# Attention and feed-forward layer on one core: the pooled result added to the windows by GpSimd's accumulating transfers instead of a load and a tensor_add, with the planner's durations and leads set anew

## The chip, the core and the metric

The program runs on one core of a Trainium2 chip. A core has a matrix engine (TensorE, PE in the profile), a vector engine (VectorE, DVE), a scalar engine (ScalarE, ACT), GpSimd (POOL), a queue engine that only issues transfers (SyncE, SP), and 16 DMA engines that carry the transfers. Each engine runs its own list of instructions in order; engines wait for one another through semaphores alone. The metric is the device time of the whole program in microseconds; less is better.

## The reference

```python
# q, k, v: (B=8, H=8, S=576, D=64)
q_d, k_d, v_d = (a.reshape(B, H, 144, 4, D).mean(axis=3) for a in (q, k, v))
out_up    = np.repeat(softmax(q_d @ k_d.T / 8) @ v_d, 4, axis=2)              # pooled attention
out_local = softmax(where(|i - j| < 4, q @ k.T / 8, -1e6)) @ v                # local attention
x  = (out_up + out_local).transpose(0, 2, 1, 3).reshape(B, S, 512)
xn = (x - mean) / sqrt(var + 1e-6) * g_ln                                     # layer norm
return x + relu(xn @ w_ch1) @ w_ch2                                           # 512 -> 2048 -> 512
```

The weights come as 64-bit floats (the program reads them as pairs of 32-bit words); the rest is fp32.

## The kernel before

**The stages.** Local attention is cut into 40 windows, 5 per batch, of 128 rows each (two stretches of 64). Pooled attention runs per batch in two halves of four heads. Where both are there, `norm(i)` makes a window's rows of x, normalizes them and turns them, and nine blocks of 512 rows (`blocks`) go through the feed-forward. The weights do not stay on chip as a whole: in a first stage ("visits" 0 to 8, one per block of rows) five eighths of the hidden width are computed by plain products, in a second stage (visits 9 to 17) the rest, by seven products in place of eight. Attention runs beside the first stage. Visit 0 also decodes the first stage's weights, and batch 0's attention comes ahead of it.

**Matmuls in three.** Each fp32 product is done as three on halves: a rounded high half (`hi`, ScalarE's cast, L407) and the rest (`lo`, VectorE's subtraction, L413 in `halved`). In the down projection (L1303, tile `acc`) the three are high weight x low activation, low weight x high, high x high. The weights' 64-bit words are first put together by `words`: ScalarE L376, VectorE L384 (`low_word`) and L387, then `halved`. A weight's `low` tile thus needs L384, L387 and L413 on VectorE before PE can use it; for w_ch2 in the first stage these are the 10 tiles `low20_0` to `low20_9`, 128 hidden columns each. `acc0_0` and `acc0_1` are the two halves (256 rows each) of visit 0's block.

**The pooled result.** `pooled(b)` loads raw tiles of q, k and v on SP (L819), GpSimd adds their groups of four rows (L832, L833), PE and the others do the attention. For batches 1 to 7 `keep` (L968) writes the result, each row four times, to the tensor `ud` in DRAM by two GpSimd transfers. (Batch 0 goes another way, through PE at L1039 and VectorE at L1048.)

**A window's norm, batches 1 to 7 (35 windows).** SP loads the window's rows of `ud` into a tile `up` (`load_up`, L1026, two transfers of 64 x 512); GpSimd adds it to the local result (`plus`, L1045, xl += up); VectorE takes the statistics (`stats`, L1052, L1054, L1055); GpSimd raises the variance to -1/2 (`rstd`, L1058, tile `mv`); VectorE normalizes (`normed`, L1062, tile `xn`); PE turns (L1070, tile `px`); ScalarE scales into the block (L1093); GpSimd writes x out for the end (`spill`, L1099, to `xs`).

**What sets the order.** `Plan` is a list scheduler that runs when the program is built. A task is added with an engine, a listed duration, a due time, what it depends on and what room it takes (`add`, L42); `order()` (L55) then takes tasks greedily by their due time as the listed durations let them begin, and so writes each engine's instructions in a fixed order. On the chip nothing of the listed times is left, only the order and the semaphores. A task with `ahead=n` may not be listed more than n us before its due time; `AHEAD` is that bound for the raw tiles' loads. `due` comes from constants such as `T0` (start of visit 0), `SHORT` (length of a second-stage visit) and `PRIOR` (how long before its batch the pooled part is due).

Of the kernel before, what the change touches and what calls it, by code (L numbers as in the profile page):

```python
# [14 lines left out]
ALU = mybir.AluOpType  # L15
# [7 lines left out]
class Plan:  # L23
# [17 lines left out]

    def add(self, eng, dur, fn, deps=(), due=0.0, take=(), give=(), lag=None, ahead=1e9, alt=None, kb=0, n=1, more=0.1, late=None):  # L42

        opts = {eng: (dur, fn, 0.0)}
        if alt is not None:
            opts[alt[0]] = alt[1:]
        t = SimpleNamespace(
            n=len(self.tasks), opts=opts, dur=dur, deps=[d for d in deps if d is not None],
            due=due, take=take, give=give, lag=lag, ahead=ahead, open=0.0, waits=0, eng=None, fn=None, kb=kb, pieces=n, more=more,
            late=late if late is not None else self.late if eng == "SP" else 0.0,  # L50
        )
        self.tasks.append(t)
        return t

    def order(self):  # L55
# [40 lines left out]
        while left:  # L96
# [61 lines left out]
def attention_then_ffn(  # L158
# [115 lines left out]
    STAGE = [sum(VISITS[i][0] != VISITS[i - 1][0] for i in range(1, v + 1)) for v in range(len(VISITS))]  # L274
    T0 = 36
    LONG0, LONG, SHORT = 75, 73, 34
    LENGTH = [LONG0 if v == 0 else LONG if FIRST[c] == v else SHORT for v, (_, c) in enumerate(VISITS)]
# [21 lines left out]
    W_NORM, G_NORM = 2.0, 9.0  # L299
    PRIOR = 30  # L300
    START = 0
# [14 lines left out]

    B0W, B0W_GAP, B0G, B0G_GAP = 5, 3, 12, 1.5
    AHEAD = 45
    U_SPARE = 4
# [21 lines left out]
    def dve(n):  # L341
        return 0.06 + n / 950.0

    def pool(n):
        return 0.13 + 0.0022 * n

    BEGUN = 1.0

# [6 lines left out]
    def words(g, which, f, due):  # L355
# [38 lines left out]
        t = add("ACT", 0.87, high_word, (t,), due)  # L394
        return add("DVE", 1.26, low_word, (t,), due, give=(("u", 2),))

    def halved(get, name, deps, more, due, keep, n=512, room=U, gone=U):

        x = SimpleNamespace()
        add = plan.add  # L400

        def high():
            x.a = get()
            if keep.get("hi") is None:
                keep["hi"] = unit([P, 512], f"hi{name}", F32R)
            x.hi = keep["hi"]
            nc.scalar.copy(x.hi[:, x.a[1]], x.a[0].bitcast(F32)[:, x.a[1]])  # L407

        def low():
            a, cols = x.a  # L410
            if keep.get("lo") is None:
                keep["lo"] = unit([P, 512], f"lo{name}", F32R)
            nc.vector.tensor_sub(keep["lo"][:, cols], a.bitcast(F32)[:, cols], x.hi.bitcast(F32)[:, cols])  # L413

        t = add("ACT", act(n, True), high, deps, due, take=room)
        return add("DVE", dve(n) * 1.4, low, [t] + more, due, take=room, give=gone)

# [134 lines left out]
    def local(i):  # L552
# [44 lines left out]
        for src, nm in () if own else ((q, "q"), (k, "k")):  # L597
# [20 lines left out]
            else:  # L618
# [9 lines left out]
                for jb in range(2):  # L628
                    ts.append(add("SP", 1.95, lambda src=src, nm=nm, jb=jb: load_blocks(src, nm, jb, nc.sync), ts,
                                  due - 14.0, take=() if jb else U, lag=LAT, kb=200, n=4, more=0.8, ahead=AHEAD,  # L630
                                  alt=("ACT", 3.2, lambda src=src, nm=nm, jb=jb: load_blocks(src, nm, jb, nc.scalar), LATER) if i >= ALSO else None))
# [236 lines left out]
    def pooled_pair(b, hg, pr, x, ready):  # L868
# [126 lines left out]
        if own or pr == 0:  # L995
            return
        t = add("POOL", 2 * BEGUN, keep, x.od_done, due, lag=LAT, kb=640, n=2, more=0.6)
        ud_done.setdefault(b, []).append(t)
# [14 lines left out]
    def norm(i):  # L1013
# [7 lines left out]

        def load_up():
            x.up = unit([P, DM], f"up{i}")
            for par in range(2):
                t0 = window_start(w, par)
                nc.sync.dma_start(x.up[64 * par : 64 * par + 64], ud[b][t0 : t0 + 64])  # L1026

# [4 lines left out]
        def expand():  # L1032
            x.up = psa(f"ex{i}")
            for hg in range(2):
                es = slice(hg * 256, (hg + 1) * 256)
                for par in range(2):
                    for c in cover(par):
# [4 lines left out]
                        )  # L1042

        def plus():
            nc.gpsimd.tensor_add(xl(), xl(), x.up)  # L1045

# [423 lines left out]
```

## Time and profile before

| what | value |
|---|---|
| runs | 1038.08, 1036.22, 1039.69 us, median 1038.08 |
| the profiled execution | 1032.09 us, its span 1030.4 us |
| mean granted TensorE clock of the profiled execution | 0.996 of full speed |
| busy share of the span | PE 98%, VectorE 64%, ScalarE 44%, GpSimd 45% |

The profile is one execution, 0.6% under the median of the runs. The span runs from the first to the last instruction; about 1.7 us lie around it. Busy time of an engine says how long its instructions were at work; where an instruction stood for a semaphore, the trace names the instruction or transfer that released it. A granted clock of 1.00 is 2.4 GHz, 0.50 is 1.2 GHz.

### The profile page before, as it was taken

The numbers are of one execution on the slowest core, as the hardware profiler recorded it, in microseconds if no ns is written. First come the engines' busy times: TensorE is split into PE (matmuls) and PEld (weight loads), VectorE is DVE, ScalarE is ACT, GpSimd is POOL, SyncE is SP. The second block draws the span as 40 slices with busy tenths as digits, with TensorE's granted clock in tenths as the row PEclk, the third lists the DMA queues.
The fourth block names the chain that finished last, engine by engine and source line by source line (L and its number), as shares of the span: only waits on it lengthen the run. The fifth ranks groups of instructions, "written<-read, shape, count | busy, mean of one in ns | idle before, by whom it ended". The sixth has DMA issues, their size and how long they took to land. (4 is left out here: it accounts for less than half of the span.)

```text
span 1030.4 us, 23083 instructions
## 1 busy us (share of the span) xinstructions
PE 1008.4 (98%) x8332; PEld 854.5 (83%) x8332; DVE 664.1 (64%) x1559; ACT 449.3 (44%) x1408; POOL 463.2 (45%) x538
## 2 busy tenths in 40 slices
PE   9899989998999999999999999999999999999998
PEld 8678868887877888888888887888888999989897
DVE  6899976665765465566666554573595576556743
ACT  6587636364353464353362353653342233321311
POOL 4453567685667655664643222441244223443112
PEclk9999989999999999999999999999999999999999
DMA  7899878877878668677666241331245422344312
GB/s 181 222 271 246 197 146 217 188 185 182 200 167 198 185 141 189 150 195 162 133 175 134 74 137 60 130 135 55 86 147 184 164 91 101 137 164 164 118 63 108
DMA packets 272786, 159.24 MB, mean 155 GB/s; under 512 B 196032, under 2 KB 241344, under 8 KB 272672
## 3 DMA queue, kind: packets, MB, share of 16 engines
q1 hardware_dynamic: 249056, 119.86, 45.9%
q0 software_dynamic: 12736, 36.59, 10.5%
q10 hardware_dynamic: 10880, 1.31, 0.9%
q8 instruction: 66, 1.08, 0.4%
q14 instruction: 48, 0.39, 0.1%
HBM read 111.68 MB, written 46.01 MB: 153 GB/s over the span
## 5 line engine op out<-in xcount | busy, mean ns | idle before, releaser
L1303 PE MATMUL acc<-hiw,hl 128*128 128x512 f32 x576 | 234.5, 407 | 0.0
L1303 PE MATMUL acc<-low,hh 128*128 128x512 f32 x576 | 226.0, 392 | 5.0 <-DVE low L413 5.0
L1303 PE MATMUL acc<-hiw,hh 128*128 128x512 f32 x576 | 225.5, 392 | 0.0
L1303 PEld LDWEIGHTS acc<-hiw,hh 128*128 128x128 f32 x576 | 108.4, 188 | 24.1
L1303 PEld LDWEIGHTS acc<-low,hh 128*128 128x128 f32 x576 | 108.9, 189 | 23.0 <-DVE low L413 5.7
L1303 PEld LDWEIGHTS acc<-hiw,hl 128*128 128x128 f32 x576 | 108.6, 189 | 19.8
L1385 POOL TENSOR_TENSOR back<-back,back 128x512 f32<-128x512 f32 x36 | 48.1, 1348 | 171.1 <-DMA back<-parts 122.3
L1240 ACT ACTIVATE hh<-h 128x256 fp32r<-128x256 f32 x180 | 59.4, 386 | 144.9 <-PE h L1232 127.5
L1232 PE MATMUL h<-hix,hiw 128*128 128x512 f32 x360 | 109.5, 399 | 0.0
L1247 DVE SCALAR_TENSOR_TENSOR hl<-h,hh 128x256 fp32r<-128x256 f32 x180 | 66.9, 414 | 65.6 <-ACT hh L1240 65.2
L1283 ACT ACTIVATE hh<-e 128x256 fp32r<-128x256 f32 x108 | 39.0, 410 | 143.0 <-DVE e L1264 77.9
L1232 PE MATMUL h<-hix,low 128*128 128x512 f32 x360 | 101.1, 402 | 0.0
L1232 PE MATMUL h<-lox,hiw 128*128 128x512 f32 x360 | 97.0, 391 | 0.0
L1232 PEld LDWEIGHTS h<-lox,hiw 128*128 128x128 f32 x360 | 67.6, 188 | 15.0
L1045 POOL TENSOR_TENSOR xl<-xl,up 128x512 f32<-128x512 f32 x35 | 45.0, 1293 | 71.3 <-DMA up<-ud 21.6
L1232 PEld LDWEIGHTS h<-hix,low 128*128 128x128 f32 x360 | 64.7, 188 | 13.3 <-ACT hix L407 0.6
L1232 PEld LDWEIGHTS h<-hix,hiw 128*128 128x128 f32 x360 | 65.1, 188 | 12.6
L1093 ACT ACTIVATE xg<-px,gain 128x58 f32<-128x58 f32 (+15 forms) x280 | 61.6, 385 | 7.7 <-PE px L1070 7.6
L1264 DVE TENSOR_TENSOR e<-h,s 128x512 f32<-128x512 f32 x27 | 18.7, 691 | 69.6 <-PE h L1222 52.5
L1289 DVE SCALAR_TENSOR_TENSOR hl<-e,hh 128x256 fp32r<-128x256 f32 x108 | 57.0, 578 | 5.2 <-PE acc L1303 3.4
L1058 POOL TENSOR_TENSOR mv<-mv,neg_half 128x1 f32<-128x1 f32 x40 | 23.9, 601 | 47.6 <-DVE mv L1055 38.7
L1099 POOL DMA_DIRECT2D xs<-xl x80 | 44.6, 563 | 0.0
(249 smaller groups left out, 2068.9 us busy)
## 6 DMA issues: line engine op xcount, KB each, us to landing
s<-in_moe_w_ch_dram SPq DMA_DIRECT2D x64, 256.0 KB
blocks<-xg POOLq DMA_DIRECT2D x36, 256.0 KB, 4.3
parts<-part POOLq DMA_DIRECT2D x36, 256.0 KB, 4.1
xf_B<-blocks SPq DMA_DIRECT2D x36, 256.0 KB
back<-xs SPq DMA_DIRECT2D x36, 256.0 KB
back<-parts SPq DMA_DIRECT2D x36, 256.0 KB
out_dram<-back SPq DMA_DIRECT2D x36, 256.0 KB
up<-ud SPq DMA_DIRECT2D x70, 128.0 KB
```

Source lines behind the costliest of these rows:

```text
L1045: nc.gpsimd.tensor_add(xl(), xl(), x.up)
L1058: nc.gpsimd.tensor_tensor(x.mv[:, 1:2], x.mv[:, 1:2], neg_half, op=ALU.pow)
L1093: nc.scalar.activation(to, at, AF.Copy, scale=gain[:, kc : kc + 1])
L1099: nc.gpsimd.dma_start(xs[q0 : q0 + n], xl()[r0 : r0 + n])
L1232: nc.tensor.matmul(y.ps[fi], lhsT=wt[a][:, kc * P : (kc + 1) * P], rhs=xx[b], start=n == 0, stop=n == 3 * KC - 1)
L1240: nc.scalar.activation(hh[v, p, th][:, 256 * fi : 256 * fi + 256], side(fi, th), AF.Relu)
L1247: nc.vector.scalar_tensor_tensor(out=hl[v, p, th][:, fs], in0=side(fi, th), scalar=0.0, in1=hh[v, p, th][:, fs].bitcast(F32), op0=ALU.max, ...
L1264: nc.vector.tensor_add(two(y.e1), two(y.ps[1]), both(y.s))
L1283: nc.scalar.activation(hh[v, p, th][:, 256 * fi : 256 * fi + 256], place(th, fi), AF.Relu)
L1289: eng.scalar_tensor_tensor(out=hl[v, p, th][:, fs], in0=place(th, fi), scalar=0.0, in1=hh[v, p, th][:, fs].bitcast(F32), op0=ALU.max, op1= ...
L1303: nc.tensor.matmul(acc[v, th][j], lhsT=lt[:, ts], rhs=rt, start=p == 0 and fi == 0 and n == 0, stop=p == npr - 1 and fi == 1 and n == 2,)
L1385: nc.gpsimd.tensor_add(y.x, y.x, y.p)
```

## The change

Three things, in one edit.

1. `load_up` and GpSimd's `tensor_add` go, with the tile `up`. In their place `plus` is two GpSimd transfers with `accum_op=ALU.add`, from `ud` straight onto `xl`. They depend on `ud` and on the local result, and the rest of `norm` follows as before.
2. The planner gets an argument `port`: where GpSimd is listed as busy when a task is taken, the task's listed duration grows by `port`. It is 0.9 for `low_word` and 0.4 for `halved`, whose plain listed duration falls from 1.4 to 1.15 of `dve(n)`. Listed durations of issues are set anew: `BEGUN` (one GpSimd issue) 1.0 to 0.56, `keep` 2.0 to 1.48, SP's block loads 1.95 to 2.0.
3. Constants of due times: `T0` 36 to 42, `SHORT` 34 to 30, `PRIOR` 30 to 35, `B0W` 5 to 0, `AHEAD` 45 to 30, `DC` 1.2 to 0.8.

```diff
+            if engines["POOL"] > r + 0.2:
+                t.dur += t.port
...
-    BEGUN = 1.0
+    BEGUN = 0.56
...
-        return add("DVE", 1.26, low_word, (t,), due, give=(("u", 2),))
+        return add("DVE", 1.26, low_word, (t,), due, give=(("u", 2),), port=0.9)
...
-        return add("DVE", dve(n) * 1.4, low, [t] + more, due, take=room, give=gone)
+        return add("DVE", dve(n) * 1.15, low, [t] + more, due, take=room, give=gone, port=0.4)
...
-        t = add("POOL", 2 * BEGUN, keep, x.od_done, due, lag=LAT, kb=640, n=2, more=0.6)
+        t = add("POOL", 1.48, keep, x.od_done, due, lag=LAT, kb=640, n=2, more=0.6)
...
-        def load_up():
-            x.up = unit([P, DM], f"up{i}")
+        def plus():
             for par in range(2):
+                hs = slice(64 * par, 64 * par + 64)
                 t0 = window_start(w, par)
-                nc.sync.dma_start(x.up[64 * par : 64 * par + 64], ud[b][t0 : t0 + 64])
+                nc.gpsimd.dma_start(xl()[hs], ud[b][t0 : t0 + 64], accum_op=ALU.add)
...
-        def plus():
-            nc.gpsimd.tensor_add(xl(), xl(), x.up)
...
-            t = add("SP", 1.1, load_up, ud_done[b], due - 4.0, take=U, kb=270, n=2, more=0.6, ahead=12.0)
-            t = kept = add("POOL", pool(512), plus, [t] + outs, due - 3.0, give=U)
+            t = kept = add("POOL", 2 * BEGUN, plus, ud_done[b] + outs, due - 4.0, lag=LAT, kb=400, n=2, more=0.6)
```

In the changed file the lines up to `norm` stand two lower (L413 is L415, L968 is L970), the new transfer is L1028, and what follows stands one to two higher (L1052 is L1051, L1058 is L1057, L1062 is L1061, L1303 is L1301).

By number, the instructions differ in little: GpSimd has 35 tensor_adds less and 70 transfer issues more, SP 70 issues less, and PE 69 filler groups (L216, matmuls of the identity) in place of 74. The order differs in much. Three places follow.

**VectorE, end of visit 0**, where the last two low halves of w_ch2's first block are made (`low20_8`, `low20_9`); `hl` is an activation's low half, `st`, `mv`, `xn` are the steps of batch 1's windows 5 to 8. Before:

```order
L1247 SCALAR_TENSOR_TENSOR hl0_4_0_2292<-h0_4_1_2267,hh0_4_0_2255 128x256
L1247 SCALAR_TENSOR_TENSOR hl0_4_1_2294<-h0_4_1_2267,hh0_4_1_2257 128x256
L413 TENSOR_TENSOR low20_8_2325<-cva0_2_8_2201,hiw20_8_2279 128x512
L413 TENSOR_TENSOR low20_9_2343<-cva0_2_9_2228,hiw20_9_2323 128x512
L911 TENSOR_REDUCE gmx4_0_2409<-gs4_0_2392 96x3
```

and with the change:

```order
L1051 BN_STATS st7_2363<-xl7_1939 128x6
L1053 BN_AGGR mv7_2365<-st7_2363 128x2
L1054 TENSOR_SCALAR mv7_2365<-mv7_2365 128x1
L1061 TENSOR_SCALAR xn5_2377<-xl5_1475,mv5_2314 128x512
L415 TENSOR_TENSOR low20_8_2379<-cva0_2_8_2221,hiw20_8_2274 128x512
L415 TENSOR_TENSOR low20_9_2387<-cva0_2_9_2242,hiw20_9_2325 128x512
L1051 BN_STATS st8_2416<-xl8_2285 128x6
```

Before, the statistics of windows 5 to 8 all stand behind the two low halves; now those of 5, 6 and 7 and window 5's `normed` stand ahead of them, and the pair of `hl` stands behind.

**PE at the same place**, up to the first use of `low20_8`. Before:

```order
L1303 MATMUL acc0_0_1_1647<-hiw20_7_2037,hh0_3_0_1983 128x512
L711 MATMUL lt9_2327<-ident_66,la9_2307 128x128 x4
L1303 MATMUL acc0_1_0_2332<-hiw20_0_1362,hl0_0_1_1367 128x512
L1303 MATMUL acc0_1_0_2332<-low20_0_1382,hh0_0_1_1348 128x512
L1303 MATMUL acc0_1_0_2332<-hiw20_0_1362,hh0_0_1_1348 128x512
L1303 MATMUL acc0_1_1_2333<-hiw20_0_1362,hl0_0_1_1367 128x512
L1303 MATMUL acc0_1_1_2333<-low20_0_1382,hh0_0_1_1348 128x512
L1303 MATMUL acc0_1_1_2333<-hiw20_0_1362,hh0_0_1_1348 128x512
L1303 MATMUL acc0_0_0_1646<-hiw20_8_2279,hl0_4_0_2292 128x512
L1303 MATMUL acc0_0_0_1646<-low20_8_2325,hh0_4_0_2255 128x512
```

and with the change:

```order
L1301 MATMUL acc0_1_0_2184<-hiw20_7_2050,hl0_3_1_2008 128x512
L1301 MATMUL acc0_1_0_2184<-low20_7_2099,hh0_3_1_1990 128x512
L1301 MATMUL acc0_1_0_2184<-hiw20_7_2050,hh0_3_1_1990 128x512
L1301 MATMUL acc0_1_1_2185<-hiw20_7_2050,hl0_3_1_2008 128x512
L1301 MATMUL acc0_1_1_2185<-low20_7_2099,hh0_3_1_1990 128x512
L1301 MATMUL acc0_1_1_2185<-hiw20_7_2050,hh0_3_1_1990 128x512
L909 MATMUL gs4_1_2469<-ktg4_1_2451,qbdg1_81 96x144 x3
L1301 MATMUL acc0_0_0_1555<-hiw20_8_2274,hl0_4_0_2217 128x512
L1301 MATMUL acc0_0_0_1555<-low20_8_2379,hh0_4_0_2206 128x512
```

Before, PE had done 6 matmuls of the block's second half (`acc0_1`, weight 0) when it came to `low20_8`; now it has done 48, up to weight 7.

**GpSimd around the first of `ud`'s writes for batch 1 that windows wait for.** Before:

```order
L832 TENSOR_TENSOR raw4v0_2316<-raw4v0_2316 72x4x128
L833 TENSOR_TENSOR vd0_82<-raw4v0_2316 72x4x64
L1045 TENSOR_TENSOR xl5_1519<-xl5_1519,up5_2320 128x512
L1045 TENSOR_TENSOR xl6_1662<-xl6_1662,up6_2340 128x512
L1045 TENSOR_TENSOR xl7_1886<-xl7_1886,up7_2349 128x512
L1045 TENSOR_TENSOR xl8_2223<-xl8_2223,up8_2358 128x512
L832 TENSOR_TENSOR raw4v1_2396<-raw4v1_2396 72x4x128
```

and with the change:

```order
L970 DMA ud1_1424<-od3_2043 288x1x256 x2
L834 TENSOR_TENSOR raw4k0_2024<-raw4k0_2024 72x4x128
L835 TENSOR_TENSOR kd4_2136<-raw4k0_2024 72x256
L1028 DMA xl5_1475<-ud1_1424 64x512 x2
L1028 DMA xl6_1660<-ud1_1424 64x512 x2
L1028 DMA xl7_1939<-ud1_1424 64x512 x2
L834 TENSOR_TENSOR raw4q1_2125<-raw4q1_2125 72x4x128
L835 TENSOR_TENSOR qd4_2061<-raw4q1_2125 72x256
L1028 DMA xl8_2285<-ud1_1424 64x512 x2
```

Before, six pooling instructions stand between the write of `ud1` and these rows, and four tensor_adds follow one another; now the first adding transfer is two instructions behind the write. In later batches (`xl20`, `xl25`, `xl30`, `xl35`) it stands right behind it.

## Rows read from the trace of the kernel before

**Rows 1.** The page's first part: the span, and each engine's busy time, share of the span and number of instructions.

```profile
span 1030.4 us, 23083 instructions
PE 1008.4 (98%) x8332; PEld 854.5 (83%) x8332; DVE 664.1 (64%) x1559; ACT 449.3 (44%) x1408; POOL 463.2 (45%) x538
```

**Rows 2.** The waits of PE over the whole span: what waited for what, us in total, times, the longest in us.

```profile
PE acc L1303 <- DVE low L413: 5.0, 2, 3.8
PE gt L926 <- ACT ag L920: 2.7, 3, 1.9
PE gs L907 <- ACT ktg L893: 1.9, 2, 1.4
...
PE gq L880 <- POOL kd L833: 1.4, 1, 1.4
PE gv L943 <- POOL vd L833: 1.3, 1, 1.3
```

**Rows 3.** The span by stretches: start and end, length, then busy us (and instructions) of PE, PE's weight loads, VectorE, ScalarE and GpSimd, the granted clock, the DMA engines' busy share and GB/s.

```profile
75.00:100.00 25.00, 25.00 (x270) 20.28 (x263) 23.93 (x57) 19.57 (x61) 9.54 (x9) 1.00 0.93 247
100.00:125.00 25.00, 24.99 (x256) 21.65 (x255) 24.45 (x57) 15.86 (x48) 13.00 (x12) 1.00 0.88 203
125.00:150.00 25.00, 20.02 (x138) 16.54 (x137) 19.19 (x36) 7.47 (x22) 16.96 (x18) 0.86 0.75 157
775.00:1025.00 250.00, 250.00 (x1553) 225.90 (x1552) 150.87 (x259) 64.64 (x158) 75.02 (x58) 1.00 0.37 129
```

**Rows 4.** L413 on VectorE, first the two of 125 to 140 us, then all 26 that write a weight's `low` tile: shortest, middle and longest in ns, first and last start in us, the form.

```profile
L413 DVE TENSOR_TENSOR low<-cva,hiw x2: 1712/3910/6109, 129.8 to 131.5; 128x512 fp32r<-128x512 f32 x2
...
L413 DVE TENSOR_TENSOR low<-cva,hiw x26: 669/681/6109, 58.2 to 764.0; 128x512 fp32r<-128x512 f32 x26
```

**Rows 5.** The timeline of GpSimd at that place: start in us, us, the instruction (x counts neighbours told together).

```profile
129.71 1.27 POOL L832 TENSOR_TENSOR raw4v<-raw4v 72x512 f32<-72x512 f32 x1 [1.10 <-DMA raw4v<-in_v_dram]
131.06 1.06 POOL L833 TENSOR_TENSOR vd<-raw4v 72x256 f32<-72x256 f32 x1
132.08 4.93 POOL L1045 TENSOR_TENSOR xl<-xl,up 128x512 f32<-128x512 f32 x4
```

**Rows 6.** The timeline of PE, behind the wait at 137.6 us and then 35 us later, where the same 12 small matmuls (`gs`) run again; in brackets the idle time before a row and what ended it.

```profile
137.62 0.79 PE L1303 MATMUL acc<-low,hh 128*128 128x512 f32 x1 [3.83 <-DVE low L413]
...
139.92 2.83 PE L907 MATMUL gs<-ktg,qbdg 128*96 128x144 f32 x12
...
173.46 1.63 PE L907 MATMUL gs<-ktg,qbdg 128*96 128x144 f32 x12
```

**Rows 7.** Stretches of 2 us at that place, columns as in rows 3: the granted clock is the third number from the end.

```profile
136.00:138.00 2.00, 0.38 (x1) 0.38 (x2) 1.57 (x1) 0.00 (x0) 2.00 (x2) 0.50 1.12 195
142.00:144.00 2.00, 2.00 (x40) 1.67 (x39) 1.55 (x5) 0.91 (x3) 0.00 (x0) 0.91 0.51 75
```

**Rows 8.** The chain that ended last, one piece of it: start in us, us, 24 matmuls of the down projection back to back.

```profile
768.13 5.47 PE acc L1303 x24
```

**Rows 9.** Groups of instructions by line: line, engine, operation, tile, count, busy us in all, mean ns of one, idle time of the engine just before them and what ended it.

```profile
L1045 POOL TENSOR_TENSOR xl<-xl,up 128x512 f32<-128x512 f32 x35 | 45.0, 1293 | 71.3 <-DMA up<-ud 21.6 <-ACT xl L759 15.3 <-PE gq L880 11.4
L754 DVE TENSOR_TENSOR xl<-lv,lr 64x256 f32<-64x256 f32 x92 | 38.1, 414 | 1.2
L1052 DVE BATCH_NORM_STATS2 st<-xl 128x6 f32<-128x512 f32 x40 | 27.4, 684 | 6.6 <-POOL xl L1045 6.4
L1054 DVE BATCH_NORM_AGGREGATE mv<-st 128x2 f32<-128x6 f32 x40 | 7.3, 182 | 1.4
L1055 DVE TENSOR_SCALAR mv<-mv 128x1 f32<-128x1 f32 x40 | 6.2, 154 | 1.4
L1058 POOL TENSOR_TENSOR mv<-mv,neg_half 128x1 f32<-128x1 f32 x40 | 23.9, 601 | 47.6 <-DVE mv L1055 38.7 <-DMA kr<-in_k_dram 5.1 <-DMA qr<-in_q_dram 3.3
L1062 DVE TENSOR_SCALAR xn<-xl,mv 128x512 f32<-128x512 f32 x40 | 23.4, 597 | 4.3 <-POOL mv L1058 3.0 <-ACT hh L1240 0.7 <-PE acc L1303 0.3
```

**Rows 10.** Issues of transfers by line: GpSimd's of x to `xs` (the nearest shape to the new ones), GpSimd's of the pooled result to `ud` with the time from issue to landing, and SP's of `up`: count, shortest, middle and longest issue in ns, first and last start in us.

```profile
L1099 POOL DMA_DIRECT2D xs<-xl x80: 518/547/782, 38.7 to 661.7; - x80
...
L968 POOL DMA_DIRECT2D ud<-od x28: 687/751/822, 74.1 to 589.3; - x28
...
DMA to landing us min/median/max: 3.4/4.9/8.3
...
L1026 SPq DMA_DIRECT2D up<-ud x70: 444/587/1439, 125.2 to 599.9; - x70
```

**Rows 11.** What VectorE's transposes of q and k (L622) stood waiting for, us and times: the transfers of the local windows.

```profile
  DMA kr<-in_k_dram: 14.5, 9
  DMA qr<-in_q_dram: 6.9, 7
```

**Rows 12.** The end of visit 0 on PE and ScalarE: the last turns of block 1, the first up-projection of visit 1, the scaling and the casts between them.

```profile
152.55 1.92 PE L1070 MATMUL px<-ident,xn 128*128 128x128 f32 x16
...
160.64 1.07 PE L1232 MATMUL h<-hix,low 128*128 128x512 f32 x4
...
153.19 5.23 ACT L1093 ACTIVATE xg<-px,gain 128x58 f32<-128x58 f32 x24 [0.60 <-PE px L1070]
...
158.13 2.36 ACT L407 CAST hix<-xg 128x512 fp32r<-128x512 f32 x4
```

More of the change, by code (lines that the diff above doesn't have):

```diff
@@ L40, in __init__, with add @@
         self.landed, self.soft = [], []
-    def add(self, eng, dur, fn, deps=(), due=0.0, take=(), give=(), lag=None, ahead=1e9, alt=None, kb=0, n=1, more=0.1, late=None):
+    def add(self, eng, dur, fn, deps=(), due=0.0, take=(), give=(), lag=None, ahead=1e9, alt=None, kb=0, n=1, more=0.1, late=None, port=0.0):
         opts = {eng: (dur, fn, 0.0)}
@@ L48, in add @@
             n=len(self.tasks), opts=opts, dur=dur, deps=[d for d in deps if d is not None],
-            due=due, take=take, give=give, lag=lag, ahead=ahead, open=0.0, waits=0, eng=None, fn=None, kb=kb, pieces=n, more=more,
+            due=due, take=take, give=give, lag=lag, ahead=ahead, open=0.0, waits=0, eng=None, fn=None, kb=kb, pieces=n, more=more, port=port,
             late=late if late is not None else self.late if eng == "SP" else 0.0,
@@ L274, in attention_then_ffn @@
     STAGE = [sum(VISITS[i][0] != VISITS[i - 1][0] for i in range(1, v + 1)) for v in range(len(VISITS))]
-    T0 = 36
-    LONG0, LONG, SHORT = 75, 73, 34
+    T0 = 42
+    LONG0, LONG, SHORT = 75, 73, 30
     LENGTH = [LONG0 if v == 0 else LONG if FIRST[c] == v else SHORT for v, (_, c) in enumerate(VISITS)]
@@ L299, in attention_then_ffn @@
     W_NORM, G_NORM = 2.0, 9.0
-    PRIOR = 30
+    PRIOR = 35
     START = 0
@@ L315, in pooled_at @@
         return g_base + b * ROUND - (NPAIR - 1 - pr) * (ROUND / NPAIR if b > 1 else G1)
-    B0W, B0W_GAP, B0G, B0G_GAP = 5, 3, 12, 1.5
-    AHEAD = 45
+    B0W, B0W_GAP, B0G, B0G_GAP = 0, 3, 12, 1.5
+    AHEAD = 30
     U_SPARE = 4
@@ L628, in local @@
                 for jb in range(2):
-                    ts.append(add("SP", 1.95, lambda src=src, nm=nm, jb=jb: load_blocks(src, nm, jb, nc.sync), ts,
+                    ts.append(add("SP", 2.0, lambda src=src, nm=nm, jb=jb: load_blocks(src, nm, jb, nc.sync), ts,
                                   due - 14.0, take=() if jb else U, lag=LAT, kb=200, n=4, more=0.8, ahead=AHEAD,
@@ L1356, in attention_then_ffn @@
     DB = 5.8
-    DC = 1.2
+    DC = 0.8
     DOWN = (((DA, 0.5), (DB, 0.5)), ((DC, 1.0), (DC, 1.0)))
```

## The prediction

> **What bounds the kernel now.** Read the page's first part: PE is busy 98% of the span, the next engine 64% [rows 1]. Then the stretches [rows 3]: in the last one, 250 us of the second stage, PE is busy for all 250.00. Nothing can be gained there; a gain has to come from the 22 us (1030.4 - 1008.4) in which PE stands, or from stretches at half clock. Third, the waits of PE [rows 2]. The largest by far is the down projection standing for L413, a weight's low half on VectorE: 5.0 us in two waits. Behind it come waits on late work of attention: 2.7 and 1.9 for ScalarE, 1.4 and 1.3 for GpSimd's pooled k and v.
>
> Why is L413 late? Its 26 runs take 681 ns in the middle, but two of them, at 129.8 and 131.5 us, take 1712 and 6109 [rows 4]. GpSimd pools v from 129.71 and adds xl += up four times from 132.08 to 137.0 [rows 5]; the 6.1 us instruction begins at 131.5, and PE goes on at 137.62 [rows 6], right behind the last add. So the adds hold the weight's decoding. The reader should see one more thing: from 75 to 125 us VectorE is busy 24 of every 25 us [rows 3], so it comes to `low20_8` and `low20_9` with no lead, whatever GpSimd does.
>
> **The stall costs more than its waits.** Behind it the granted clock is 0.50, the lower level, where it had been 1.00, and it is 0.91 in the stretch from 142 [rows 7]. Five wide matmuls from 137.62 to 139.92 take 2.30 us [rows 6]; at full clock one takes 5.47 / 24 = 0.228 [rows 8], five 1.14. The 12 `gs` behind take 2.83 against 1.63 later [rows 6]. Loss: 1.16 + 1.20 = 2.4 us.
>
> **The change part by part.**
>
> *The order around `low20_8`.* PE now comes to it after 48 matmuls of `acc0_1` in place of 6, so 42 x 0.228 = 9.6 us later on PE than before, counted from weight 7. Part of that is no new lead: the matmuls of the last hidden pair (12, 2.7 us) stood ahead in the old order and fall into this stretch in the new. That leaves about 7. On VectorE the two low halves move the other way: three statistics (0.684 + 0.182 + 0.154 = 1.02 each) and one `normed` (0.597) now stand ahead [rows 9], 3.7 us, and the pair of `hl` goes behind. Net lead about 4 to 5 us over the old order, and the four adds that held them are gone. I take the stall at zero: **-5.0** for the waits **-2.4** for the clock. Its new condition: VectorE now waits there for an adding transfer and for GpSimd's `mv`, ahead of weights that PE needs.
>
> *GpSimd's work.* 35 x 1.293 = 45.0 us of adds go [rows 9]. 70 issues come; the trace has no adding issue, and I take the nearest in shape, rows of x of 512 columns to `xs`, 547 ns [rows 10]: 38 us. GpSimd is at 45% [rows 1], the sum is off the path. The old adds also stood 71.3 us idle, 21.6 of them for `up` [rows 9]; now GpSimd stands for `ud`'s own landing (median 4.9, longest 8.3 [rows 10]) wherever the adding transfer is right behind the write, as at `xl20`, and the raw tiles' pooling queues behind it. The nearest rows of what that costs are PE's waits for pooled k and v, 1.4 and 1.3 [rows 2]. Bounds: nothing, or one such wait in five batches, 5 x 1.4 = 7. I take one more: **+1.4**. It could gain nothing itself.
>
> *SP.* 70 issues go, 70 x 0.587 = 41 us of its queue [rows 10]; the loads behind them go out earlier. SP's loads reach PE through none of the large waits in rows 2, so I cost it at nothing.
>
> *A window's chain.* Before: landing of `up`, add, statistics. Now: two issues (1.1), landing, statistics (1.02), `mv` (0.601), `normed` (0.597) [rows 9, 10], and ahead of it the divide, about 1.5 by L754's 0.414, two to three a window: 4.8 us and the landing L. In the new order the tightest distance on PE from a window's `lv` to its `px` is window 26's: 42 wide matmuls (9.6 us), 12 turns at 1.92 / 16 = 0.12 [rows 12] and 30 small ones, 12 us together. The chain fits for L up to 12 - 4.8 = 7.2. For L no row exists; the bounds are `ud`'s shortest 3.4, and, since an add has to read its target as well, twice its median, 9.8 [rows 10]. Nearest is `ud`'s median itself, 4.9: it fits, **0**.
>
> *Start of visit 1.* From the first of the last turns, at 152.55, PE came to the first up-projection after 8.1 us, and the scaling and the cast of the four operands were through after 158.13 + 2.36 - 152.55 = 7.9 [rows 12]: just in time. In the new order the work between is 16 turns (1.7), 12 wide matmuls (2.7) and small ones and fillers (2.5 by my count), 6.9 us; the fourth operand is wanted three matmuls later, at 7.6, and comes at 7.9: **+0.3**.
>
> *Less lead and the other numbers.* Raw tiles may be listed 30 us ahead of due, not 45. The local tiles' transfers, the ones that are late already (VectorE's transposes stand 14.5 and 6.9 us for them [rows 11]), hardly show in PE's waits. `port` and the durations act only through the order. Fillers fall from 74 to 69: nothing.
>
> **Sum:** -5.0 - 2.4 + 1.4 + 0.3 = -5.7 us. The profiled execution's 1032.09 us (6.0 below the median) becomes 1026.4; against the median, 1038.08 - 5.7 = **1032.4 us**. About 0.3%, 3.1 us, is what a measurement of this kernel can tell from no change.
>
> **The rivals.**
>
> *1. The adding transfers land late (slower).* Point of decision: L above 7.2 us. With L = 9.8, window 26 is 12 + 2.6 late, and each batch has a window nearly as tight; GpSimd, which runs in order, carries the lateness on to the raw tiles. Seven batches at 2 to 3 us give +14 to +21, so 1032.4 + 14 to 21 = 1046 to 1053. For it: an add moves its bytes twice, and the DMA engines are 93% busy at 75 to 100 us and still 75% when the first of them starts [rows 3]. Against it: the median of a larger transfer is 4.9. On adding transfers the Trainium skill ("DMA: Bandwidth & Descriptors", section Rules for kernel authors) says that they read the destination and write it later, with nothing holding the bytes in between; no run of before shows one.
>
> *2. The stall moves and is not removed (no change).* VectorE has no lead in visit 0 [rows 3], and now statistics that hang on a landing stand ahead of the weights. A landing 4 to 5 us later than I think brings the 5.0 + 2.4 back: 1038.08 + 1.4 + 0.3 - 0 to 4, about 1038.
>
> *3. The other late work goes too (faster).* With SP relieved and GpSimd 7 us lighter the waits for k, v, `ag`, `ktg` (1.4 + 1.3 + 2.7 + 1.9 = 7.3 [rows 2]) shrink, and my +1.4 does not come: 1032.4 - 8.7 = 1023.7. Against: most of these hang on ScalarE.
>
> *4. VectorE starves the issues.* If a busy VectorE held GpSimd's issues to several times their time, each window's two would take 2 x 2.5 us longer, past the 7.2 - 4.9 = 2.3 that window 26 has: 2.7 late, as rival 1, some 1050. In the trace 80 such issues take at most 782 ns [rows 10] with VectorE at 95% for tens of us. The rule stands in the Trainium skill ("SBUF — State Buffer", section SBUF: two separate sides, the trap in which VectorE blocks GpSimd's transfers, and 620 against 3100 ns in the section behind it). By it 70 issues would cost 70 x 2.5 = 174 us more of GpSimd (an estimate from that page); the trace so far disagrees with it for this kernel.
>
> **How the numbers follow.** Forecast 0.47, rival 1 0.17, rival 2 0.23, rival 3 0.10, rival 4 0.03. The forecast's own range is 1031 (no new wait) to 1038 (five of them). The tails: rival 3 below, 1021 if a little more goes; half of rival 1 is let out above, so 1046. Faster by over 0.3% (under 1035): 0.42 of the forecast, 0.10 of rival 3, 0.02 of rival 2, 0.54. Same: 0.05, 0.18 of rival 2, 0.02 of rival 1: 0.25. Slower: 0.15 of rival 1, 0.03 of rival 2, 0.03 of rival 4: 0.21.
>
> **What would show it.** Right: no wait of `acc` for L413's successor (L415) around 130 to 140 us, granted clock 1.00 there, L415's longest far under 6.1 us; 70 issues of about 0.55 us on GpSimd; landings near 5 us; PE's waits for `px` and pooled tiles within 2 us. Wrong: PE standing for `low` again at the end of visit 0 with VectorE's `st` waiting for the transfer just before (rival 2); repeated waits of `px` for `xn` through batches 2 to 7 (rival 1); adding issues of 2 us and more (rival 4).

## The result and the profile after

The change made the kernel slower: 1042.42 us median of 20 runs (1035.64 to 1047.48) against 1037.14 of before (1028.13 to 1044.68); the ratio of the runs is 1.0069, 95% interval 1.0047 to 1.0091, so 5 to 9 us more. (The ratio is not the quotient of the two medians, 1.0051; the interval holds both.) The forecast was 1032.4, its own range 1031 to 1038: the time moved the other way, into the part to which the prediction gave 0.21. All ratios below are to the kernel before on the same chip; single runs spread over some 15 us, so it is the ratio and its interval that count, and a profile's own time may lie 5 us off. The profiled execution of after took 1041.6 us (span 1039.9), 0.8 under its median; that of before lies 5.0 under the median of its 20 runs.

First the line that answers to [rows 1]:

```profile
span 1039.9 us, 23038 instructions
PE 1013.8 (97%) x8322; PEld 855.7 (82%) x8322; DVE 683.3 (66%) x1557; ACT 450.4 (43%) x1416; POOL 485.6 (47%) x573
```

GpSimd (POOL) was to get 7 us less work and has 22.4 more (485.6 - 463.2). The stretches of [rows 3], and the `low` row of [rows 4]:

```profile
75.00:100.00 25.00, 25.00 (x251) 20.30 (x251) 21.64 (x57) 18.71 (x62) 10.01 (x10) 1.00 0.98 247
100.00:125.00 25.00, 25.00 (x216) 21.02 (x216) 24.17 (x54) 17.52 (x54) 13.57 (x14) 1.00 0.81 193
125.00:150.00 25.00, 25.00 (x215) 21.29 (x213) 20.77 (x46) 11.50 (x36) 20.77 (x27) 1.00 0.87 159
```

```profile
L415 DVE TENSOR_TENSOR low<-cva,hiw x26: 648/682/1426, 60.7 to 774.6; 128x512 fp32r<-128x512 f32 x26
```

From 125 to 150 us PE is now busy for all 25.00 us at full clock, where it was 20.02 at 0.86; the longest `low` takes 1.43 us in place of 6.1. The stall is gone as forecast. What came instead stands in PE's waits, to be read beside [rows 2]:

```profile
PE gt L928 <- ACT ag L922: 3.4, 2, 3.0
PE gq L882 <- POOL kd L835: 3.0, 2, 2.5
PE h L1220 <- DVE e L1262: 2.4, 1, 2.4
PE lv L734 <- ACT at L720: 2.1, 3, 0.9
...
PE h L1230 <- ACT hix L409: 1.6, 1, 1.6
...
PE h L1230 <- DVE lox L415: 1.4, 2, 0.7
PE px L1069 <- DVE xn L1061: 1.1, 1, 1.1
```

No wait is as large as the old one; there are more of them. The 200 us behind visit 0, before and then after, show it in one row each (busy us of PE first, the granted clock third from the end):

```profile
150.00:350.00 200.00, 194.50 (x1771) 159.29 (x1770) 124.24 (x343) 98.37 (x345) 133.83 (x162) 1.00 0.80 189
```

```profile
150.00:350.00 200.00, 190.51 (x1764) 155.00 (x1762) 135.13 (x343) 94.75 (x336) 136.28 (x166) 0.99 0.87 188
```

PE stands 4.0 us more there. (With plain transfers in the same order it is busy as long as before, below.) And a wait costs more than itself: behind the 2.98 us in which PE stood for `ag`, until 289.01, the granted clock is 0.50, the lower level, from 290 to 293 us, and 1.00 again from 294:

```profile
290.00:291.00 1.00, 1.00 (x4) 0.81 (x4) 0.75 (x2) 0.61 (x3) 0.00 (x0) 0.50 1.10 156
292.00:293.00 1.00, 1.00 (x14) 0.38 (x16) 0.39 (x1) 0.00 (x0) 0.96 (x1) 0.50 0.24 38
294.00:295.00 1.00, 1.00 (x15) 0.96 (x14) 0.59 (x3) 0.00 (x0) 0.35 (x1) 1.00 0.67 143
```

The new transfers, and the group rows that answer to [rows 9] and [rows 10]:

```profile
L1028 POOL DMA_DIRECT2D xl<-ud x70: 812/914/2359, 122.9 to 662.3; - x70
...
DMA to landing us min/median/max: 3.0/5.0/7.9
```

```profile
L1028 POOL DMA_DIRECT2D xl<-ud x70 | 60.3, 1048 | 63.5 <-PE h L1230 18.0 <-issue 17.9 <-DMA ud<-od 12.5
L1098 POOL DMA_DIRECT2D xs<-xl x80 | 51.2, 705 | 1.7 <-issue 1.7
L1051 DVE BATCH_NORM_STATS2 st<-xl 128x6 f32<-128x512 f32 x40 | 27.4, 684 | 33.5 <-DMA xl<-ud 32.7 <-ACT la L704 0.6
```

The landing is what I took (5.0 us, longest 7.9). The issue is not: 914 ns in the middle where I took 547. The mean of 1048 and the longest of 2359 need care: where issues follow one another their records overlap, and together they cover 60.3 us, 0.86 for each of the 70. So 60.3 us of issues replace 45.0 us of adds.

### The profile page after: what moved, and what is told of

It reads as the page before. It is cut to its first block, busy times and chain, and to the rows that moved or that the text cites. A ratio compares the mean times of both kernels' runs of the same rounds, so it can differ in the third digit from the quotient of the medians.

```text
span 1039.9 us, 23038 instructions
## 1 busy us (share of the span) xinstructions
PE 1013.8 (97%) x8322; PEld 855.7 (82%) x8322; DVE 683.3 (66%) x1557; ACT 450.4 (43%) x1416; POOL 485.6 (47%) x573
## 2 busy tenths in 40 slices
DMA packets 272785, 159.23 MB, mean 153 GB/s; under 512 B 196032, under 2 KB 241344, under 8 KB 272672
## 3 DMA queue, kind: packets, MB, share of 16 engines
q0 software_dynamic: 18336, 45.77, 16.1%
## 4 chain that ended last, share of the span: by engine, by line
PE 81%; DMA 10%; DVE 3%; SPq 2%; ACT 2%; issue 1%; POOL 1%; POOLq 0%; DVEq 0%; ACTq 0%
PE acc L1301 32%; PE h L1230 20%; PE h L1220 13%; PE gv L945 2%; DMA vwin<-in_v_dram 2%; PE gs L909 2%; PE lv L734 2%; PE lt L713 2%; PE gt L928 1%; PE ls L678 1%; DMA kr<-in_k_dram 1%; DMA raw8v<-in_v_dram 1%; SPq L568 1%; PE px L1069 1%; ACT xg L1092 1%
## 5 line engine op out<-in xcount | busy, mean ns | idle before, releaser
L1301 PE MATMUL acc<-hiw,hl 128*128 128x512 f32 x576 | 234.3, 407 | 0.0
L1301 PE MATMUL acc<-hiw,hh 128*128 128x512 f32 x576 | 225.5, 392 | 0.0
L1301 PE MATMUL acc<-low,hh 128*128 128x512 f32 x576 | 225.5, 391 | 0.0
L1301 PEld LDWEIGHTS acc<-hiw,hh 128*128 128x128 f32 x576 | 108.4, 188 | 24.1
L1301 PEld LDWEIGHTS acc<-hiw,hl 128*128 128x128 f32 x576 | 108.8, 189 | 20.5
L1301 PEld LDWEIGHTS acc<-low,hh 128*128 128x128 f32 x576 | 108.9, 189 | 18.6
L1230 PE MATMUL h<-hix,low 128*128 128x512 f32 x360 | 103.2, 406 | 1.7 <-ACT hix L409 1.6
L1028 POOL DMA_DIRECT2D xl<-ud x70 | 60.3, 1048 | 63.5 <-PE h L1230 18.0
L1287 DVE SCALAR_TENSOR_TENSOR hl<-e,hh 128x256 fp32r<-128x256 f32 x108 | 63.2, 628 | 3.1 <-ACT hh L1281 2.8
L1098 POOL DMA_DIRECT2D xs<-xl x80 | 51.2, 705 | 1.7 <-issue 1.7
L1057 POOL TENSOR_TENSOR mv<-mv,neg_half 128x1 f32<-128x1 f32 x40 | 25.6, 641 | 55.2 <-DVE mv L1054 53.3
```

The source lines that it names most:

```text
L1028: nc.gpsimd.dma_start(xl()[hs], ud[b][t0 : t0 + 64], accum_op=ALU.add)
L1057: nc.gpsimd.tensor_tensor(x.mv[:, 1:2], x.mv[:, 1:2], neg_half, op=ALU.pow)
L1098: nc.gpsimd.dma_start(xs[q0 : q0 + n], xl()[r0 : r0 + n])
L1230: nc.tensor.matmul(y.ps[fi], lhsT=wt[a][:, kc * P : (kc + 1) * P], rhs=xx[b], start=n == 0, stop=n == 3 * KC - 1)
L1287: eng.scalar_tensor_tensor(out=hl[v, p, th][:, fs], in0=place(th, fi), scalar=0.0, in1=hh[v, p, th][:, fs].bitcast(F32), op0=ALU.max, op1= ...
L1301: nc.tensor.matmul(acc[v, th][j], lhsT=lt[:, ts], rhs=rt, start=p == 0 and fi == 0 and n == 0, stop=p == npr - 1 and fi == 1 and n == 2,)
```

## The experiments

Three theories stand behind the expectations. Theory 1: the adding transfers themselves cost, through GpSimd's time. Theory 2: the constants give a worse order. Theory 3: any new order brings its own small waits. Each experiment ran beside the kernel before.

**The parts alone and in pairs.** a stands for the transfers (point 1 of the change), b for `port` and the listed durations (point 2), c for the constants (point 3). The edits are those pieces of the change's diff and nothing else.

> Only the adding transfers; durations and constants as before. Theory 1 (the transfers themselves cost: an issue takes 0.91 to 1.05 us in place of 0.55, GpSimd comes later to all else): slower than before by 5 to 12 us, as much as the whole change or more. Theory 2 (the constants T0 to DC move the order to a worse one): not slower, -6 to +1 us, since the stall of 5.0 + 2.4 us at the end of visit 0 goes with the adds. Theory 3 (any new order has new small waits): between -5 and +8 us, and the waits lie at other places than in the changed kernel.

> The load on SP and GpSimd's tensor_add stay; port, listed durations and constants are the change's. Theory 1: faster than before by 3 to 8 us, the transfers alone having cost the gain. Theory 2: slower by 3 to 10 us, like the whole change. Theory 3: anything between, with waits at other places.

> Only the constants T0, SHORT, PRIOR, B0W, AHEAD, DC. Theory 1: within 3 us of before. Theory 2: slower by 5 to 12 us. Theory 3: anything between, with waits at other places.

> Adding transfers with port and the listed durations; the constants T0 to DC as before. If it is the durations (a GpSimd issue listed at 0.56 us where an adding one takes 0.91 and more) that fit badly with the transfers: 1040 to 1045 us. If it is the constants (less lead for the raw tiles): 1032 to 1037.

> Adding transfers with the constants T0 to DC; port and durations as before, so an issue is listed at 1.0 us. The other way round from e9: by the durations 1032 to 1037 us, by the constants 1040 to 1045. If it is the order as such and no single part, neither holds for both.

> port and the listed durations alone, with the load on SP and GpSimd's tensor_add and the constants as before: the last corner of the eight combinations. If the durations are bad only together with the transfers: 0.997 to 1.004 of before. If they are bad by themselves: 1.006 to 1.014, as with the transfers.

| parts | run | ratio | 95% interval |
|---|---|---|---|
| a | e1 | 0.9974 | 0.9948 to 1.0001 |
| b | e18 | 1.0085 | 1.0051 to 1.0120 |
| c | e3 | 0.9997 | 0.9972 to 1.0022 |
| a, b | e9 | 1.0111 | 1.0060 to 1.0161 |
| a, c | e10 | 1.0041 | 1.0010 to 1.0072 |
| b, c | e2 | 1.0000 | 0.9972 to 1.0028 |
| a, b, c | the change | 1.0069 | 1.0047 to 1.0091 |

Averaged over the four pairs that differ by one part alone, a costs 0.28%, (-0.26 + 0.26 + 0.44 + 0.69) / 4; b 0.63%, (0.85 + 1.37 + 0.03 + 0.28) / 4; c gains 0.16%. The parts don't add up. The transfers come out 0.26% faster in the old order and slower in the three others, but only beside b and c (0.69%) do the intervals stand apart. Theory 2 falls as it was put, since c by itself is neutral; yet c costs 0.67% on top of a (e1 to e10) and gains 0.85% on top of b (e18 to e2), both with intervals apart. Theory 1 fails as it was put, since a alone is not slower. With a, both b (e9) and c (e10) cost, the third of e10's cases. And the case in which b would be harmless without a didn't come: b costs 0.85% by itself. e18 shows where:

```profile
PE gq L882 <- POOL kd L835: 4.8, 4, 2.1
PE h L1224 <- DVE e L1266: 3.1, 1, 3.1
PE lt L713 <- ACT la L704: 2.8, 1, 2.8
PE gt L928 <- ACT ag L922: 2.3, 2, 1.5
```

```profile
150.00:350.00 200.00, 189.17 (x1700) 154.15 (x1701) 128.77 (x339) 92.42 (x320) 134.01 (x163) 0.97 0.82 191
```

Waits of the same kinds as in the change (`kd`, `e` and `ag` are in its list too), and from 150 to 350 us 5.3 us less of PE than before at a mean clock of 0.97, without any adding transfer. In all these kernels the stall at the end of visit 0 is gone or small (no `low` wait in e18 and e2, 1.8 us in e3, 1.7 in e10, where it was 5.0), so losing it is no mark of the transfers: any of the three parts moves the order enough.

**The adding taken away, the order kept.** e4 and e11 have every instruction where it stands in the change and in e1; only the flag goes.

```diff
-                nc.gpsimd.dma_start(xl()[hs], ud[b][t0 : t0 + 64], accum_op=ALU.add)
+                nc.gpsimd.dma_start(xl()[hs], ud[b][t0 : t0 + 64])
```

> The changed kernel with the same order of instructions on every engine, but the 70 transfers write the rows of ud onto xl without adding (the local result is lost). Theory 1, if the adding is what costs: issues fall from 0.91 to 0.55 us, 26 us less on GpSimd, and the time by 3 to 8 us against the changed kernel (1042.4 to about 1036). Theories 2 and 3: within 2 us of the changed kernel.

> e1 (only the transfers, old planner) with plain transfers in place of adding ones (the local result is lost), the order as in e1. If the adding costs in every order as it does in the change's (9 us): 1025 us, 0.9885 of before. If e1's order has room on GpSimd for it: within 3 us of e1, 0.995 to 0.999.

e4: 0.9982 (0.9952 to 1.0013). Against the change's 1.0069 that is 0.87% or 9 us, a little more than expected, intervals apart. e11: 0.9943 (0.9915 to 0.9972) against e1's 0.9974: 3 us, intervals overlapping. So adding costs 9 us in the change's order and at most about as much in e1's, where 3 is the likeliest. The transfers in e4:

```profile
L1028 POOL DMA_DIRECT2D xl<-ud x70: 516/539/721, 121.8 to 652.9; - x70
...
DMA to landing us min/median/max: 2.3/4.3/7.0
```

An issue is 0.375 us shorter in the middle (the 70 cover 37.9 us in place of 60.3, 22 less), a landing 0.7 us. The issues to `xs`, which often stand right behind, cover 46.0 us in e4 and 51.2 in the change: they are longer too. From 150 to 350 us PE is busy as long as before:

```profile
150.00:350.00 200.00, 194.44 (x1813) 157.99 (x1812) 135.90 (x355) 97.16 (x343) 130.08 (x169) 1.00 0.84 188
```

Since PE's order is the same, the two traces can be laid over each other matmul by matmul. This is how much later than in e4 a matmul of the change starts, at the steps of over 0.4 us (worked out from both traces). The first adding transfer is issued at 122.86 us; the 0.65 us by which the change is late at 125 us were there before any transfer could tell:

```
start    later by  step   what PE waited for there in the change
45.95    0.89      +0.79  vwin
55.05    0.97      +0.84  ktg  (partly made good: 0.65 at 125)
164.50   1.35      +0.69  kd
198.52   3.20      +1.76  kd
272.97   2.97      +0.50  vd
289.01   4.03      +1.02  ag   (6.10 by 311.7: the half clock behind it, and lox)
311.69   6.10      +0.52  lox
366.97   7.10      +1.00  at
382.63   8.33      +1.21  xn
768.11   8.71      -0.58  (in e4 PE waits there)
```

Three of the steps behind 125 us are pooled tiles that GpSimd makes (`kd`, `vd`), one is the window's own chain (`xn`).

Where it begins shows at the first adding transfers: GpSimd's timeline, with one row of SP's, in the change and then in e4.

```profile
122.86 5.11 POOL L1028 DMA_DIRECT2D xl<-ud  x6 [2.52 <-DMA ud<-od]
129.37 0.81 POOL L835 TENSOR_TENSOR qd<-raw4q 72x256 f32<-72x256 f32 x1
130.20 0.31 SPq L821 DMA_DIRECT2D raw4v<-in_v_dram  x1
```

```profile
121.78 3.28 POOL L1028 DMA_DIRECT2D xl<-ud  x6 [2.03 <-DMA ud<-od]
126.45 0.80 POOL L835 TENSOR_TENSOR qd<-raw4q 72x256 f32<-72x256 f32 x1
127.28 0.31 SPq L821 DMA_DIRECT2D raw4v<-in_v_dram  x1
```

Six issues take 5.11 us in place of 3.28. The transfers start 1.1 us later than in e4, `qd` 2.9, and SP, which stands until `qd` is done with its raw tile, issues the next raw tile's load 2.9 later, with its other loads behind. From there to 200 us SP's loads go out 1.9 to 5.3 us later than in e4. The step at 198.5, where PE meets it, GpSimd's timeline in the change and then in e4:

```profile
183.88 1.29 POOL L834 TENSOR_TENSOR raw6k<-raw6k 72x512 f32<-72x512 f32 x1 [4.46 <-DMA raw6k<-in_k_dram]
...
188.77 0.73 POOL L835 TENSOR_TENSOR qd<-raw6q 72x256 f32<-72x256 f32 x1
190.24 3.42 POOL L1028 DMA_DIRECT2D xl<-ud  x4 [0.74 <-DMA ud<-od]
192.41 2.36 POOL L1098 DMA_DIRECT2D xs<-xl  x2
196.41 1.25 POOL L834 TENSOR_TENSOR raw6k<-raw6k 72x512 f32<-72x512 f32 x1 [1.64 <-DMA raw6k<-in_k_dram]
```

```profile
179.64 1.28 POOL L834 TENSOR_TENSOR raw6k<-raw6k 72x512 f32<-72x512 f32 x1 [3.61 <-DMA raw6k<-in_k_dram]
...
185.90 0.73 POOL L835 TENSOR_TENSOR qd<-raw6q 72x256 f32<-72x256 f32 x1
187.43 2.15 POOL L1028 DMA_DIRECT2D xl<-ud  x4 [0.81 <-DMA ud<-od]
...
193.18 1.28 POOL L834 TENSOR_TENSOR raw6k<-raw6k 72x512 f32<-72x512 f32 x1 [2.54 <-DMA raw6k<-in_k_dram]
```

The second `raw6k` starts 6.9 us behind the end of `qd` in the change (196.41 - 189.50) and 6.6 in e4 (193.18 - 186.63): it follows `qd` at nearly the same distance, so it is late because `qd` is. The four longer issues between them (3.42 us, 2.15 in e4) are not what holds it here: behind them GpSimd still stands 1.64 us for the load. The chain that ended last says why:

```profile
189.17 0.95 SPq L585
...
190.52 5.81 DMA raw6k<-in_k_dram
...
196.41 1.26 POOL raw6k L834
...
197.74 0.73 POOL kd L835
...
198.52 0.53 PE gq L882 x5
```

There are only two raw tiles (`NSTG` = 2). SP (which here was at L585, another load, for 0.6 us more) can issue the next load when GpSimd has done with one, the load takes 5.8 us, and GpSimd needs it at once. SP stood 42.9 us for GpSimd's `qd`, `kd`, `vd` in the change (20.0 + 14.3 + 8.6) and 20.0 before:

```profile
SPq L821 <- POOL qd L835: 20.0, 8, 4.8
SPq L821 <- POOL kd L835: 14.3, 7, 5.9
SPq L821 <- POOL vd L835: 8.6, 6, 2.6
```

That is the way by which an engine that is busy for 47% of the span holds PE: lateness on GpSimd is lateness of the next load. (In e4 the three come to 38.5 us, so most of this was there without the adding, from the order; in e1, which is not slower than before, to 35.0. The sum is no price by itself.)

**More and less of GpSimd's time.** e5 puts three memsets behind each plain transfer; e13 takes the 80 issues to `xs` away.

```diff
-                nc.gpsimd.dma_start(xl()[hs], ud[b][t0 : t0 + 64], accum_op=ALU.add)
+                nc.gpsimd.dma_start(xl()[hs], ud[b][t0 : t0 + 64])
+                for _ in range(3):
+                    nc.gpsimd.memset(pad, 0.0)        # e5; pad is 128 x 40
...
-                nc.gpsimd.dma_start(xs[q0 : q0 + n], xl()[r0 : r0 + n])        # e13
```

> As e4 (plain transfers in the changed kernel's order), with three small GpSimd memsets behind each transfer, some 0.35 us, so that GpSimd is about as long at each transfer as with adding. If the issue's length on GpSimd is what adding costs (0.91 against 0.54 us): the time goes back to that of the changed kernel, 1039 to 1043 us. If the landing of the adding transfer (5.0 against 4.3 us) or the traffic is what costs: it stays near e4, 1032 to 1036.

> The changed kernel in its order, without the 80 issues of x to xs on GpSimd (51 us of it); the end reads the input v in place of xs, so the residual is left out. If GpSimd's time between the pooled tiles is what the change ran into (26 us less gave 9 us in e4): 1024 to 1034 us. If it is the landing of the adding transfers or the order alone: 1039 to 1044.

e5: 1.0134 (1.0103 to 1.0166), 15.8 us over e4 and 6.7 over the change, more than expected. The memsets take 29.7 us:

```profile
L1031 POOL MEMSET pad<- 128x40 f32 x210 | 29.7, 141 | 8.0
```

e13: 0.9986 (0.9952 to 1.0019), 8.6 us under the change, as expected. With e4 that makes three kernels in one order: 22 us less, 51 less and 30 more of GpSimd move the time by -9, -9 and (from e4) +16 us. The sign is always GpSimd's; the price per us is not constant, 0.4, 0.2 and 0.5, and e5's GpSimd is busy only 3.7 us longer than the change's (489.3 against 485.6), so the place of the time counts and not only its sum. e13's gain may not be GpSimd's alone: without the 80 transfers the DMA engines also move 9.4 MB less (149.78 against 159.23). e5 has no such second difference from e4. It has e4's short landings (4.5 us) and is the slowest of these kernels, so GpSimd's time alone is enough to lose what the adding loses, and theory 1 holds in the change's order. That the landing, 0.7 us longer with adding, has no share in the 9 us is not shown.

**One transfer a window.** e7 (in the change) and e8 (in e1) read both stretches of 64 rows by one pattern of three dimensions.

```diff
-            for par in range(2):
...
+            src = bass.AP(tensor=a.tensor, offset=a.offset, ap=[[(t1 - t0) * DM, 2], [DM, 64], [1, DM]])
+            nc.gpsimd.dma_start(xl(), src, accum_op=ALU.add)
```

> The changed kernel with one adding transfer of 128 x 512 a window in place of two of 64 x 512; the same listed durations, so the same order. GpSimd issues 35 in place of 70. If the issue time is what costs: 1.0 to 1.4 us for one against 1.83 for two, 15 to 30 us less on GpSimd, and 1034 to 1039 us. If the landing costs: within 2 us of the changed kernel.

> e1 (the adding transfers alone, old durations and constants) with one transfer a window. If issue time costs there too: 1 to 4 us under e1's 0.9974 of before; if the plan of e1, which lists 2.0 us, already hides it: within 1.5 us of e1.

1.2341 and 1.2196, against both expectations. In e7 the issue did get cheaper (1.43 us for one against 2 x 0.91), but the landing is three times as long:

```profile
L1028 POOL DMA_DIRECT2D xl<-ud x35: 1351/1432/2692, 119.9 to 882.9; - x35
...
DMA to landing us min/median/max: 13.8/15.0/20.9
```

```profile
q0 software_dynamic: 49136, 46.02, 14.1%
```

GpSimd's queue moved 49136 packets in place of 18336. The rows themselves are not cut any smaller: by the traces' packet records both kernels carry them in 4480 packets of 2048 bytes, and what is more in e7 is packets of 8 bytes, 896 to a transfer. But where such a transfer is alone (25 of the 35), its 128 packets of 2048 bytes run at most 3 or 4 at a time; in the change up to 12 to 22 of that size run at once. As an experiment on the issue it failed. It does show that a long landing hurts: with 10 us more of it the time is 1278.6 - 1042.4 = 236 us longer, 6.7 for each of 35 windows. Rival 1's mechanism is thus real at 13.8 us and more; what a landing between the change's longest, 7.9, and that would cost no run shows.

**Single numbers of the planner.**

```diff
-            t = kept = add("POOL", 2 * BEGUN, plus, ...
+            t = kept = add("POOL", 2.0, plus, ...          # e6
...
-    AHEAD = 30
+    AHEAD = 45                                             # e14
```

> The changed kernel with one number of the planner other: a window's two adding transfers are listed with 2.0 us of GpSimd, as they measure (2 x 0.91 and more), in place of 1.12. If the plan is wrong because it lists them too short, so that GpSimd falls behind the plan: the gain comes back, 1032 to 1037 us. If the adding costs in any order: 1040 to 1044.

> The changed kernel with AHEAD back at 45, so that raw tiles may be listed 45 us ahead of their due time. If less lead is what costs: 1032 to 1037 us. If the two raw tiles' own turn (loaded only when GpSimd has freed one) sets when they are loaded, lead changes nothing of itself: 1038 to 1048, as any new order.

e6: 1.0119 (1.0086 to 1.0153), some 5 us over the change although the listed number is nearer to the measured one; PE stands 8.1 us for `kd` in it, 7.6 of them at once. e14: 1.0032 (0.9999 to 1.0064), some 4 us under the change: less lead is a part of the cost at most. Both intervals overlap the change's. As far as they tell, one number moves the time by 4 or 5 us through the order, as theory 3 has it.

**A third raw tile.**

```diff
-    NU, NSTG = 87, 2
+    NU, NSTG = 85, 3
```

> The changed kernel with three raw tiles in place of two (and 85 general tiles in place of 87, which is the same memory). If the turn of two raw tiles through SP's load, GpSimd's adds and back is where GpSimd's longer issues come to bear: 1030 to 1037 us. If not: 1040 to 1050.

> e1 (adding transfers alone, old durations and constants) with three raw tiles and 85 general ones. By the turn of the raw tiles: 2 to 6 us under e1, 0.991 to 0.996 of before. If two tiles are enough in that order: within 3 us of e1 or slower for the two tiles that are gone.

1.0254 (1.0206 to 1.0301) and 1.0136 (1.0099 to 1.0173): slower, both. The plan has two general tiles less and another order, and SP still stands for GpSimd's raw tiles (26.1 us in e15, 42.9 in e16). It doesn't tell whether the turn of two tiles would loosen with memory to spare; that stays open.

**Issues given to another engine.** e12: the 80 issues to `xs` on SP, in the change. e17: the 36 issues to `blocks` on ScalarE, in e1.

```diff
-                nc.gpsimd.dma_start(xs[q0 : q0 + n], xl()[r0 : r0 + n])
+                nc.sync.dma_start(xs[q0 : q0 + n], xl()[r0 : r0 + n])      # e12
...
-                    nc.gpsimd.dma_start(blocks[c, kc], block[c, kc])
+                    nc.scalar.dma_start(blocks[c, kc], block[c, kc])       # e17
```

> The changed kernel with its order on PE, VectorE and ScalarE; only the 80 issues of x to xs go from GpSimd (51 us of it) to SP. If GpSimd's time between the pooled tiles is the bound that the change ran into: 1028 to 1037 us. If not, or if SP's loads come later by it: 1040 to 1050.

> e1 (adding transfers alone, old planner) with its order; the 36 issues of the first visits' blocks, some 20 us, go from GpSimd to ScalarE, which has just written what they send. If GpSimd's time counts in e1's order as it does in the change's (26 us for 9): 3 to 7 us under e1, 0.991 to 0.995 of before. If ScalarE's own work is as tight, or e1's order has room: 0.996 to 1.003.

e12: 1.0882 (1.0837 to 1.0927), and e13 shows that the same issues taken away altogether gain 8.6 us: what costs is that SP, in order, stands for the windows' x with the loads behind it (61.4 us in 13 waits for `xl<-ud` to land). e17: 1.0037 (1.0004 to 1.0069), some 6 us over e1; the issue is short there (340 ns), but PE's waits for ScalarE's `ktg` grow from 2.5 to 6.0 us. Both were to be gains and are misses. e11's time, 0.9943, needs transfers that don't add. e1, the transfers without the planner's part, is the best complete version: ahead of the change, and 0.9974 of before with an interval that just reaches 1.

## Why the prediction was wrong, point by point

**The stall around `low20_8`: right.** It went, clock and all: 75 to 150 us cost PE nothing in idle time. Of the two reasons given, the order and the adds that are gone, the order is enough by itself: e18 and e2 keep the adds and have no such wait.

**GpSimd's work: the step that failed.** "GpSimd is at 45%, the sum is off the path" took the busy share for the limit, and 547 ns, an issue without adding, for the price. Measured, an issue is 914 ns in the middle, the 70 take 22 us more of GpSimd than e4's plain ones, and adding costs 9 us in this order in place of the +1.4 (bounds 0 to 7). I had the way: the raw tiles' pooling queues behind. I did not follow it on to SP's load, which waits for the tile, and back. The sign "PE's waits for `px` and pooled tiles within 2 us" failed too: 3.0 us for `kd`, 2.5 of them at once.

**SP, less lead, `port` and durations at nothing: wrong as a sum.** Plain transfers with the old planner, which is what the forecast priced, gain 5.9 us (e11; interval 3 to 9) where it had -5.7; so close a match is partly luck, since its terms were not measured one by one. Plain transfers with the new numbers gain 1.9 (e4). So the order that the numbers make costs some 4 us (the two intervals overlap), and b alone 8.8 (e18). I had looked at the order only where the stall was. e4 has that order without the adding, and its new waits stand elsewhere: 1.64 us for `hix` at 64.6 us, the first up-projection of visit 0, and 2.36 for `e` at 764.8, where before has 0.87. Along this path the parts are -5.9 for e11, +4.0 from e11 to e4 and +9.0 from e4 to the change, 7.1 together (7.2 is 0.69% of 1037). They must add up, being three steps between the same ratios; by another path (e2, then the transfers) they would be 0 and 7.2.

**A window's chain: right but for one window.** Landing 5.0 against 4.9 taken; `px` waits 1.1 us once for `xn`, the step of 1.2 at 382.6 where the prediction had 0. The start of visit 1 (+0.3) shows no wait in PE's list that answers to it; its sum also took 1.7 us for 16 turns for which the row has 1.92, and with that the term is about 0.1.

**The rivals.** Rival 1 had the side and the place (GpSimd in order, the raw tiles) with the wrong cause: landings were below its 7.2 us in the middle (longest 7.9), and the adding cost 9 us where it had 14 to 21. Rival 2: the weights' wait did not come back, but other waits did. Rival 3 went the other way: `kd` 1.4 to 3.0, `ag` 2.7 to 3.4. Rival 4: a few issues reach 2.36 us, the median is far from it, and the longest stand at the end of a row of issues, as the sixth of the six at 122.86, whose records overlap; plain issues in the same order stay under 0.73, so the rule as the Trainium skill tells it ("SBUF — State Buffer", section SBUF: two separate sides) is not what made these longer. What in the adding makes an issue 0.37 us longer was not tried. One difference is on record: GpSimd's queue moves 16096 packets in e4 and 18336 in the change, 32 more for each of the 70 transfers, because the rows go in packets of 2048 bytes where the plain transfers have 4096. That this is what makes the issue longer is not shown.

## What to carry to other kernels

An engine's busy share doesn't say that its time is free: where it frees a buffer for which the next load waits, and there are two such buffers, part of each us of it can reach the bound engine whatever its share (0.2 to 0.5 of it in one order here; perhaps less in e1's). Price a new form of transfer by a row of that form or with a wide bound, the issue on the issuing engine apart from the landing. And where a planner writes the order, a new number is a new order: change the mechanism with the order held fixed, and measure the planner's numbers by themselves.

## What was not expected of the hardware

- An adding issue on GpSimd takes 914 ns in the middle against 539 for the same transfer without adding, in the same place of the same order (0.86 against 0.54 us each by the time that the 70 cover); the landing is 5.0 against 4.3 us, and the data go in packets of 2048 against 4096 bytes.
- One adding transfer of 128 x 512 whose source has an outer dimension of 2 takes 15.0 us to land, two of 64 x 512 take 5.0 each. Alone, it has at most 3 or 4 packets of 2048 bytes under way at a time, against up to 12 to 22 in the change. Source and target changed together, so which of them does it is not shown.
- 0.42 us of memsets behind each of 70 transfers (29.7 us in all) made the whole 15.8 us longer.
